# Feed-forward in row tiles of 64: the products with w1 and w3 side by side in two phases, the product with w2 in two parts, transposes in halves

## The chip, the cores and the metric

The kernel runs on one core of a Trainium2 chip. The metric is the device time of one execution in microseconds (us); three runs of the kernel before gave a median of 1179.75 us (1178.96 to 1179.86). A core has TensorE (PE in the profile; PEld is its weight load), VectorE (DVE), ScalarE (ACT), GpSimd (POOL) and SyncE (SP), which here only issues DMAs. Each engine works through its own instructions in the order of the program; between engines there are semaphores. Matrix products go to PSUM, eight banks of 128 partitions by 512 fp32 values, from which ACT and DVE read.

## The reference

A transformer block on x of 2048 rows by D = 448, 16 heads of 28 with one shared key and value, and a gated feed-forward of width F = 1792.

```python
x = A_x
h = x + _A_ref(_layernorm(x, axis=-1), A_wq, A_wk, A_wv, A_wo)
h2 = h + _B_ref(_layernorm(h, axis=-1), B_w1, B_w3, B_w2)

def _B_ref(x, w1, w3, w2):
    gate = jnp.einsum("bsd,df->bsf", x, w1)
    up = jnp.einsum("bsd,df->bsf", x, w3)
    h = _silu(gate) * up
    return jnp.einsum("bsf,fd->bsd", h, w2)
```

`_A_ref` is softmax attention over all 2048 keys; `_layernorm` has no gain or bias.

## The kernel before

**Numbers.** Operands of large products are fp32 values split into a rounded part and a remainder of the type fp32r (names ending in h and l, or index 0 and 1). A product is then three matmuls: high by high, low by high, high by low. D = 448 is three blocks of 128 and one of 64. For the last block the transposed input `xh[:, 3]` holds the low part in partitions 0 to 63 and the high part in 64 to 127, and the weights hold the same 64 rows twice, so that two matmuls over all 128 partitions do what three halves ask for. A product over D is thus 3 x 3 + 2 = 11 matmuls (`mm_D`, line 156).

**Stages.** The attention takes the span up to about 742 us; the change leaves its instructions alone on every engine. Then comes the feed-forward: 4 row tiles of T = 512 rows (t) by 14 chunks of 128 hidden columns (k), 56 iterations. One iteration, in the order in which the engines get it:

- `split_w(k+2)`: DVE copies the raw w1 and w3 of a later chunk into fp32r (line 442), POOL makes the remainder (line 443). The results are the tiles `qs`.
- `ffn1(t, k)`, line 970: two products of 11 matmuls, first w1 by the normalised input (`xh`, `xl`) into a bank `pa`, then w3 into another. Then the **hidden chain**: ACT Silu of the first bank (line 975), DVE multiplies with the second (977), ACT rounds the result (980), DVE makes the remainder (981). The tiles are `pt`, from a ring of four.
- what the table `after` hangs on this place: normalising the rows of the next tile (DVE, line 210), their transposes (`ln_tr`, line 238, 4 matmuls of 128x128 on PE, then ACT line 240 and DVE line 247), and in the first tile the last rows of the attention's output product (`wo_rows`).
- `ffn2` of the iteration before, line 989: 4 row blocks (n) by 3 matmuls of 128x448 into four banks Y, which are summed over all 14 chunks of a row tile.
- after chunk 0 of the next tile, `y_out` (993): DVE adds the four Y banks to the rows X, and a DMA writes them out.
- `split_w2(k+1)`: DVE line 455, POOL line 456, tiles `w2s`.

So `ffn2` of a chunk runs a whole `ffn1` later than the hidden chain that feeds it. Seven PSUM banks are handed out by `bank()`, which takes the free one that a small planner (`Clock`) expects to be ready first; the eighth (`po`) belongs to the attention.

**Row groups.** PE can be used by groups of its rows. The attention does it with 32 rows (lines 283 and 367, shown as 32*128): four matmuls, each on 32 partitions and into its own bank, follow each other within hundredths of a us. The feed-forward before uses all 128 rows (128*128) everywhere.

Of the kernel before, what the change touches and what calls it, by code (L numbers as in the profile page):

```python
# [35 lines left out]
def block_kernel(  # L36
# [18 lines left out]
    def f(ap):  # L55
        return ap.bitcast(F32)
# [81 lines left out]

    clock, ready = Clock(), {}
    free, used = list(range(7)), {}  # L140
    order = [0.0] * 7

    def bank(name="pb"):
        k = min(free, key=lambda k: order[k])
        free.remove(k)
        ps = ps_w.tile([P, T], F32, name=name, tag=f"bank{k}")
        used[id(ps)] = ps, k
        ready.pop(id(ps), None)
        return ps
# [65 lines left out]
    def xt_tiles():  # L215
        return [xt_pool.tile([P, m, T], F32R, name=name) for m, name in ((4, "xh"), (3, "xl"))]
# [11 lines left out]
    def ln_tr(t, c, spare=False):  # L228
        ps = last = TB[c] if TB else bank()
        if c == 0:  # L230
            XT[t] = xt_tiles()
        xh, xl = XT[t]
        r, c0 = (slice(0, P), c * P) if c < 3 else (slice(64, P), D - P)
        xns = LN[t][3]
        for n in range(NQ):
            if TB:
                break
            pe.transpose(ps[:, n * P : (n + 1) * P], xns[n][:, c0 : c0 + P], ident)  # L238
            clock.mm("full", 0, ps, 0.109, n == 0)
        se.activation(xh[r, c], ps[r], AF.Copy)  # L240
# [539 lines left out]
    def pt_ring():  # L780
        k, n_ring[0] = n_ring[0] % 4, n_ring[0] + 1
        return pt_new(k)
# [183 lines left out]

    HID, Y = {}, {}
    o_norm(NG - 1)

    def ffn1(t, k, W):  # L970
        ps = [bank("pa"), bank("pa")]
        for m in range(2):
            mm_D(ps[m], ps[m], [w[:, :, 1 - m] for w in W], XT[t], slice(0, P), slice(0, T))
        sg = f(pt_ring()[:, 0])
        se.activation(sg, ps[0], AF.Silu)  # L975
        done(ps[0])
        ve.tensor_tensor(sg, ps[1], sg, op=ALU.mult)  # L977
        done(ps[1])
        h = pt_ring()
        se.activation(h[:, 0], sg, AF.Copy)  # L980
        ve.tensor_tensor(h[:, 1], sg, f(h[:, 0]), op=ALU.subtract)  # L981
        HID[t, k] = h[:, 0], h[:, 1]

    def ffn2(t, k, n):
        if n == 0 and k == 0:
            Y[t] = [bank() for _ in range(NQ)]
        hid, w2s = HID[t, k], WS[t, k]
        for m, (a, b) in enumerate(((0, 0), (1, 0), (0, 1))):
            pe.matmul(Y[t][n][:, :D], hid[a][:, n * P : (n + 1) * P], w2s[:, b, :D],  # L989
                      start=(k == 0 and m == 0), stop=(k == NF - 1 and m == 2))  # L990

    def y_out(t, n):
        ve.tensor_tensor(X[t][:, n], Y[t][n][:, :D], X[t][:, n], op=ALU.add)  # L993
# [7 lines left out]
    after = {}  # L1001

    def on(t, k, fn, *args):
        after.setdefault((t, k), []).append((fn, args))

    on(0, 0.5, o_mul, tl, NG - 1)
    on(0, 2, o_split, tl, NG - 1, lambda o, i: se.activation(o, i, AF.Copy), ve)
    for k in range(2):
        on(0, 2.5, load_w13, 2 * tl + k)
    for n in range(NQ):  # L1010
        on(0, 3 + n / 2, wo_rows, tl, n)
        on(0, 5 + n, ln_stats, tl, n)
    on(0, 4.5, put_late)
    for k in range(8, NF):
# [3 lines left out]
    for t in range(1, NT):  # L1018
        for n in range(NQ):
            on(t - 1, 1 + n, ln_norm, t, n)  # L1020
        for c in range(4):
            on(t - 1, 5 + c, lambda t, c: ln_tr(t, c), t, c)

    prev = None
    for t in range(NT):
        for k in range(NF):
            end = t == tl and k >= NF - 2
            t2, k2 = divmod(NF * t + k + 2, NF)
            if t2 < NT:
                WH[t2, k2] = split_w(k2)  # L1030
            ffn1(t, k, WH.pop((t, k)))
            for fn, args in after.get((t, k), []):
                fn(*args)
            if prev is not None and not end:
# [8 lines left out]
            for fn, args in after.get((t, k + 0.5), []):  # L1043
                fn(*args)
            prev = (t, k)
    for n in range(NQ):
        ffn2(tl, NF - 3, n)
# [34 lines left out]
```

## Time and profile before

| | us |
|---|---|
| median of 3 runs | 1179.75 |
| the profiled execution | 1180.76 |
| its span | 1179.0 |
| PE busy in the span | 1168.7 |
| DVE, ACT, POOL busy in the span | 784.5, 745.1, 325.3 |
| PE busy between 900 and 1000 us (feed-forward) | 100.0 |
| DVE, ACT, POOL busy there | 37.8, 17.8, 49.4 |
| granted PE clock, mean of the span | 1.00 |

Rows of the groups view give line, engine, operation, output<-input and count, then busy time and mean ns of one, then the idle time before them and who ended it. Rows of the timeline give the start in us, the duration in us, engine, line and operation; equal neighbours are merged, with their count. A matmul's duration there is longer than the distance to the next one, because matmuls are pipelined: what counts is the distance between starts.

### The profile page before, as it was taken

The page shows a single profiled execution, that of the slowest core. Times are in us where ns is not written, and L with a number is a line of the kernel's source. Part 1 is how long each engine was busy: PE and PEld are TensorE (multiplying, and loading weights), DVE is VectorE, ACT ScalarE, POOL GpSimd, SP SyncE. Part 2 cuts the span into 40 slices and gives each one's busy share as a digit, 9 for nine tenths or more (in the row PEclk, how much of TensorE's full clock was granted, in tenths as well). Part 3 has the DMA queues.
Part 4 walks back from the last instruction along what each step waited for, and adds up shares of the span by engine and source line. Part 5 has one row for each costly group of instructions (what it writes and reads, how often), then busy time and mean ns, then how long its engine had stood idle before and what let it go on. Part 6 is the DMA issues. An engine that isn't in the chain of part 4 may idle for free.

```text
span 1179.0 us, 22184 instructions
## 1 busy us (share of the span) xinstructions
PE 1168.7 (99%) x8618; PEld 748.5 (63%) x8618; DVE 784.5 (67%) x1479; ACT 745.1 (63%) x1435; POOL 325.3 (28%) x240
## 2 busy tenths in 40 slices
PE   8999999999999999999999999999999999999998
PEld 6664444445444445444455443788888888888887
DVE  7878999897899988989987961454343333333332
ACT  5649999996999997999997999312112211211111
POOL 5312001111110111110113013335555445455552
PEclk9999999999999999999999999999999999999999
DMA  4010100011000001000011000242000000000000
GB/s 165 10 37 1 42 10 11 19 22 39 19 19 5 16 24 38 19 19 13 9 39 35 6 18 19 70 113 69 1 32 1 1 4 28 1 1 32 1 1 31
DMA packets 35049, 30.58 MB, mean 26 GB/s; under 512 B 11904, under 2 KB 29568, under 8 KB 34944
## 3 DMA queue, kind: packets, MB, share of 16 engines
q1 hardware_dynamic: 34944, 29.17, 8.6%
q8 instruction: 67, 1.10, 0.4%
q14 instruction: 38, 0.31, 0.1%
HBM read 20.37 MB, written 3.80 MB: 20 GB/s over the span
## 4 chain that ended last, share of the span: by engine, by line
PE 93%; ACT 2%; DVE 2%; DMA 1%; issue 1%; SPq 0%; POOLq 0%; POOL 0%; ACTq 0%; DVEq 0%
PE pa L163 26%; PE po L383 21%; PE pb L367 20%; PE pb L989 11%; PE pa L283 10%; PE pb L163 4%; PE pb L238 1%; ACT OT L390 1%; DVE mx L293 1%; ACT ab L304 1%; ACT pt L374 0%; DMA sd<-sm 0%; DMA X<-in_A_x_dram 0%; DVE pt L981 0%; DVE X L993 0%
## 5 line engine op out<-in xcount | busy, mean ns | idle before, releaser
L293 DVE TENSOR_REDUCE mx<-pa 128x1 f32<-128x512 f32 x689 | 440.4, 685 | 21.9 <-PE pb L367 12.9
L367 PE MATMUL pb<-qs,KS 32*128 32x512 f32 x3072 | 385.3, 425 | 0.0
L374 ACT ACTIVATE pt<-pb 128x512 f32<-128x512 f32 x684 | 365.9, 620 | 12.5 <-PE pb L367 9.4
L367 PEld LDWEIGHTS pb<-qs,KS 32*128 32x128 f32 x3072 | 233.9, 182 | 133.4 <-ACT pt L374 68.1
L283 PE MATMUL pa<-KS,qs 32*128 32x512 f32 x886 | 312.1, 459 | 1.4
L163 PE MATMUL pa<-xh,qs 128*128 128x512 f32 x896 | 231.2, 390 | 0.0
L283 PEld LDWEIGHTS pa<-KS,qs 32*128 32x128 f32 x886 | 138.9, 182 | 82.8 <-DVE mx L293 46.4
L163 PEld LDWEIGHTS pa<-xh,qs 128*128 128x128 f32 x896 | 168.1, 188 | 33.8 <-issue 0.8
L383 PE MATMUL po<-pt,VA 128*32 128x512 f32 x1368 | 182.2, 604 | 0.4 <-ACT pt L374 0.4
L977 DVE TENSOR_TENSOR pt<-pa,pt 128x512 f32<-128x512 f32 x56 | 38.7, 691 | 206.9 <-PE pa L163 202.3
L975 ACT ACTIVATE pt<-pa 128x512 f32<-128x512 f32 x56 | 33.5, 599 | 193.0 <-PE pa L163 193.0
L989 PE MATMUL pb<-w2s,pt 128*128 128x448 f32 x660 | 144.4, 367 | 1.0 <-DVE pt L981 0.8
L414 POOL TENSOR_TENSOR OT<-OT,rb 128x512 f32<-128x512 f32 x15 | 19.2, 1282 | 456.3 <-DMA rb<-sd 251.6
L980 ACT ACTIVATE pt<-pt 128x512 fp32r<-128x512 f32 x56 | 35.4, 632 | 153.6 <-DVE pt L977 149.4
L989 PEld LDWEIGHTS pb<-w2s,pt 128*128 128x128 f32 x660 | 122.9, 188 | 13.4 <-DVE pt L981 1.2
L311 DVE CUSTOM_DVE_ANT_0 ab<-pa,ab 128x512 f32<-128x512 f32 x138 | 93.7, 687 | 39.8 <-PE pa L283 32.6
L374 ACT ACTIVATE xl<-pb 128x512 f32<-128x512 f32 x170 | 99.5, 609 | 7.6 <-PE pb L367 5.5
L374 ACT ACTIVATE xh<-pb 128x512 f32<-128x512 f32 x170 | 104.2, 631 | 0.0
L163 PE MATMUL pa<-xl,qs 128*128 128x512 f32 x336 | 94.5, 389 | 0.0
L383 PE MATMUL po<-xh,VA 128*32 128x512 f32 x340 | 89.4, 605 | 0.0
L383 PE MATMUL po<-xl,VA 128*32 128x512 f32 x340 | 89.4, 605 | 0.0
L304 ACT ACTIVATE ab<-pa 128x512 f32<-128x512 f32 x138 | 82.3, 608 | 6.6 <-PE pa L283 4.8
(109 smaller groups left out, 1088.8 us busy)
## 6 DMA issues: line engine op xcount, KB each, us to landing
rb<-sd SPq DMA_DIRECT2D x64, 64.0 KB
QR<-OT SPq DMA_DIRECT2D x60, 56.0 KB
QR<-in_B_w_dram SPq DMA_DIRECT2D x16, 192.0 KB
X<-in_A_x_dram SPq DMA_DIRECT2D x3, 896.0 KB
out_dram<-X SPq DMA_DIRECT2D x3, 896.0 KB
w<-in_B_w_dram SPq DMA_DIRECT2D x8, 192.0 KB
w_wo<-in_B_w_dram SPq DMA_DIRECT2D x6, 224.0 KB
qs<-mr SPq DMA_DIRECT2D x64, 2.0 KB
```

The source lines that it names most:

```text
L163: pe.matmul(ps, lhs[b][:, cb, lsl], rhs[a][:, ca, rsl], start=(k == 0), stop=(k == len(terms) - 1),)
L283: pe.matmul(ps, QS[i][r, 0, n * P : (n + 1) * P], KS[0][r, kt * T : (kt + 1) * T] if keys is None else keys[r], start=True, stop=True)
L293: ve.tensor_reduce(self.to(), ps, axis=AX.X, op=ALU.max)
L304: se.activation(self.ab, ps, AF.Relu)
L311: ve.tensor_tensor_reduce(self.ab, ps, self.ab, 1.0, -3.0e38, ALU.add, ALU.max, self.to())
L367: pe.matmul(self.ps, KS[k % 2][r, c * P : (c + 1) * P], QS[i][r, k // 2], start=(k == 0), stop=(k == 2))
L374: se.activation(f(PT[i, c, p][:, jj]), self.ps, AF.Exp, bias=0.0, scale=SCALE)
L383: pe.matmul(PO[i][32 * j : 32 * j + 32], VA[:, c], f(PT[i, c, j // 2][:, j % 2]), start=(c == 0), stop=(c == NC - 1))
L975: se.activation(sg, ps[0], AF.Silu)
L977: ve.tensor_tensor(sg, ps[1], sg, op=ALU.mult)
L980: se.activation(h[:, 0], sg, AF.Copy)
L989: pe.matmul(Y[t][n][:, :D], hid[a][:, n * P : (n + 1) * P], w2s[:, b, :D], start=(k == 0 and m == 0), stop=(k == NF - 1 and m == 2))
```

## The change

All iterations from chunk 4 of the first row tile (`FULL = 4`) up to chunk 11 of the last, 10 + 14 + 14 + 12 = 50 of the 56, use PE in two row groups of 64. A matmul on partitions 0 to 63 and one on 64 to 127 are issued in turn (`two`).

- `ffn1` becomes an early and a late phase. Early, the lower half works on w1 into bank 0 and the upper half on w3 into bank 1; late, each half works on the other bank. The last block of D no longer needs its doubled form in each phase: early there are 11 matmuls to a half, late 10. The early phase needs the high part of the last block in partitions 0 to 63 too, which `put_xd` copies once per row tile (ACT) to a tile named `rb`.
- `ffn2` is cut the same way: early, the lower half adds to Y 0 and 2 and the upper to 1 and 3; late they swap. The order within an iteration is now ffn1 early, ffn2 early, ffn1 late, ffn2 late.
- Between the phases stands `settle`: ACT reads one element of a bank that was just written, and the matmul that next writes to that bank waits for it.
- The hidden chain starts when the late phase ends. After chunk 0 of a tile it is interrupted by the late half of `ffn2` and `y_out`.
- The transposes are done in halves of 64 rows (`tr_half`), two blocks at a time, in chunks 5 and 7 of the tile before.
- In `y_out` of the first three tiles, two of the four adds go from DVE to ACT (a copy out of PSUM, line 1078) and POOL (the add).
- The bank `po` joins the pool as an eighth bank; `wo_rows` moves from chunks 3 to 4.5 to chunks 3 and 3.5, ahead of the first half iteration.

```diff
+    free.append(7)
+    order[7] = clock.end + 4
...
+    HALF = (slice(0, 64), slice(64, 128))
+    PAIRS3 = ((0, 0), (1, 0), (0, 1))
+    FULL = 4
+    XD = {}
+
+    def put_xd(t):
+        if not XD:
+            XD[0] = wk_pool.tile([P, T], F32R, name="rb")
+        se.activation(XD[0][:64], f(XT[t][0][64:, 3]), AF.Copy)
+
+    def two(pairs):
+        for units in zip(*pairs):
+            for h, (ps, lhs, rhs, first, last) in enumerate(units):
+                pe.matmul(ps[:, : rhs.shape[-1]], lhs, rhs, start=bool(first), stop=bool(last), skip_group_check=True)
+                clock.mm("half", h, ps, 0.016 + rhs.shape[-1] / 2400, first)
+
+    def settle(ps):
+        se.activation(pexp[:1, 8:9], ps[:1, :1], AF.Copy)
+
+    def hidden(t, k, ps, then=None):
         sg = f(pt_ring()[:, 0])
         se.activation(sg, ps[0], AF.Silu)
         done(ps[0])
         ve.tensor_tensor(sg, ps[1], sg, op=ALU.mult)
         done(ps[1])
+        if then is not None:
+            then()
         h = pt_ring()
         se.activation(h[:, 0], sg, AF.Copy)
         ve.tensor_tensor(h[:, 1], sg, f(h[:, 0]), op=ALU.subtract)
         HID[t, k] = h[:, 0], h[:, 1]
...
+    def products(t, W, m, h):
+        r = HALF[h]
+        u = [(W[b][r, c, 1 - m], XT[t][a][r, c]) for a, b in PAIRS3 for c in range(3)]
+        return u + [(W[0][r, 3, 1 - m], XT[t][0][r, 3])]
+
+    def ffn1_half(t, k, W, ps, late):
+        us = [products(t, W, late, 0), products(t, W, 1 - late, 1)]
+        if not late:
+            extra = W[1][HALF[0], 3, 1], XD[0][HALF[0]]
+            us[0].insert(0 if k == NF - 1 else len(us[0]), extra)
+            us[1].append((W[1][HALF[1], 3, 0], XT[t][0][HALF[1], 3]))
+        to = (ps[0], ps[1]) if not late else (ps[1], ps[0])
+        two([[(to[h], *u, not late and x == 0, late and x == len(us[h]) - 1) for x, u in enumerate(us[h])]
+             for h in range(2)])
+        if not late:
+            settle(ps[1])
...
+    def ffn2_half(t, k, late):
+        if k == 0 and not late:
+            Y[t] = [bank() for _ in range(NQ)]
+        hid, w2s = HID[t, k], WS[t, k]
+        us = [[], []]
+        for h in range(2):
+            for n0 in (2, 0) if late else (0, 2):
+                n, r = n0 + (h ^ late), HALF[h]
+                for m, (a, b) in enumerate(PAIRS3):
+                    us[h].append((Y[t][n], hid[a][r, n * P : (n + 1) * P], w2s[r, b, :D],
+                                  not late and k == 0 and m == 0, late and k == NF - 1 and m == 2))
+        two(us)
+        settle(Y[t][0 if late else 3])
...
     def y_out(t, n):
-        ve.tensor_tensor(X[t][:, n], Y[t][n][:, :D], X[t][:, n], op=ALU.add)
+        y, eng = Y[t][n][:, :D], ve
+        if t < NT - 1 and n > 1:
+            y, eng = ln_pool.tile([P, 512], F32, name="xn", bufs=4)[:, :D], ge
+            se.activation(y, Y[t][n][:, :D], AF.Copy)
+        eng.tensor_tensor(X[t][:, n], y, X[t][:, n], op=ALU.add)
...
-            ffn1(t, k, WH.pop((t, k)))
-            for fn, args in after.get((t, k), []):
-                fn(*args)
-            if prev is not None and not end:
-                for n in range(NQ):
-                    ffn2(*prev, n)
-                if prev[1] == NF - 1:
+            W = WH.pop((t, k))
+            if t == 0 and k < FULL or end:
+                ffn1(t, k, W)
+                call(after, t, k)
+                if prev is not None and not end:
                     for n in range(NQ):
-                        y_out(prev[0], n)
+                        ffn2(*prev, n)
+            else:
+                ps = [bank("pa"), bank("pa")]
+                ffn1_half(t, k, W, ps, 0)
+                call(between, t, k)
+                ffn2_half(*prev, 0)
+                ffn1_half(t, k, W, ps, 1)
+
+                def rest():
+                    ffn2_half(*prev, 1)
+                    call(behind, t, k)
+                    if prev[1] == NF - 1:
+                        for n in range(NQ):
+                            y_out(prev[0], n)
+
+                hidden(t, k, ps, rest if prev[1] == NF - 1 else None)
+                call(after, t, k)
+                if prev[1] != NF - 1:
+                    rest()
```

**The order on PE.** The first place is an ordinary iteration of the feed-forward. Before, on PE (`pa` are the two banks of ffn1, `pb` the banks of Y, `qs` weights, `xh` and `xl` the input; 128x512 is the output of one matmul):

```order
L163 MATMUL pa<-xh,qs 128x512 x3
L163 MATMUL pa<-xl,qs 128x512 x3
L163 MATMUL pa<-xh,qs 128x512 x8
L163 MATMUL pa<-xl,qs 128x512 x3
L163 MATMUL pa<-xh,qs 128x512 x5
L989 MATMUL pb<-w2s,pt 128x448 x12
```

There are 22 matmuls of 512 columns and 12 of 448, one after the other over all rows of PE. Now, at the same place (`rb` is the copy of the last block's high part), where each matmul uses 64 rows and neighbours use different halves:

```order
L992 MATMUL pa<-xh,qs 128x512 x6
L992 MATMUL pa<-xl,qs 128x512 x6
L992 MATMUL pa<-xh,qs 128x512 x8
L992 MATMUL pa<-rb,qs 128x512
L992 MATMUL pa<-xh,qs 128x512
L992 MATMUL pb<-w2s,pt 128x448 x12
L992 MATMUL pa<-xh,qs 128x512 x6
L992 MATMUL pa<-xl,qs 128x512 x6
L992 MATMUL pa<-xh,qs 128x512 x8
L992 MATMUL pb<-w2s,pt 128x448 x12
```

In pairs these are 11 + 10 pairs of 512 columns and 6 + 6 pairs of 448; ffn2 stands in two parts, one between the phases of ffn1 and one behind.

**The order on ACT and DVE after chunk 0 of a tile.** The second place is the iteration in which the Y banks of a finished tile are read out. On DVE before (977 multiplies, 981 makes the remainder, 993 adds Y to X):

```order
L977 TENSOR_TENSOR pt<-pa,pt 128x512
L981 TENSOR_TENSOR pt<-pt 128x512
L993 TENSOR_TENSOR X_77<-pb,X_77 128x448 x4
L455 CAST w2s<-w2r_100 128x448
L442 CAST qs<-QR_89 128x1024
```

and now, with the same operations on lines 1002, 1008 and 1079:

```order
L1002 TENSOR_TENSOR pt<-pa,pt 128x512
L1079 TENSOR_TENSOR X_77<-pb,X_77 128x448 x2
L1008 TENSOR_TENSOR pt<-pt 128x512
L462 CAST w2s<-w2r_100 128x448
L449 CAST qs<-QR_89 128x1024
```

On ACT now (1000 is Silu, 996 is settle, 1078 copies Y out of PSUM, 1007 rounds the hidden tile):

```order
L1000 ACTIVATE pt<-po 128x512
L996 ACTIVATE pexp<-pb 1x1
L1078 ACTIVATE xn<-pb 128x448 x2
L1007 ACTIVATE pt<-pt 128x512
L996 ACTIVATE pexp<-pa 1x1
L996 ACTIVATE pexp<-pb 1x1
```

The remainder on DVE and the rounding on ACT, which stood ahead of the read-out of Y, now stand behind half of it each.

More of the change, by code (lines that the diff above doesn't have):

```diff
@@ L982, in ffn1 @@
         HID[t, k] = h[:, 0], h[:, 1]
+    def ffn1(t, k, W):
+        ps = [bank("pa"), bank("pa")]
+        for m in range(2):
+            mm_D(ps[m], ps[m], [w[:, :, 1 - m] for w in W], XT[t], slice(0, P), slice(0, T))
+        hidden(t, k, ps)
+    def products(t, W, m, h):
[13 more added lines that the diff above has]
+            settle(ps[1])
     def ffn2(t, k, n):
@@ L1020, in block_kernel @@
             on(t - 1, 1 + n, ln_norm, t, n)
-        for c in range(4):
-            on(t - 1, 5 + c, lambda t, c: ln_tr(t, c), t, c)
+        for p in range(2):
+            for late in range(2):
+                on(t - 1, 5 + 2 * p, tr_half, t, (2 * p, 2 * p + 1), late, to=behind if late else between)
+        on(t - 1, NF - 1, put_xd, t, to=between)
     prev = None
@@ L1042, in block_kernel @@
                 WS[t2, k2] = split_w2(k2)
-            for fn, args in after.get((t, k + 0.5), []):
-                fn(*args)
+            call(after, t, k + 0.5)
             prev = (t, k)
```

51 lines of the change are left out of this document (37 added, 14 removed).

## The prediction

> **What bounds the kernel now.** I read the page first, the engines' shares and the chain of waits:
>
> ```profile
> PE 1168.7 (99%) x8618; PEld 748.5 (63%) x8618; DVE 784.5 (67%) x1479; ACT 745.1 (63%) x1435; POOL 325.3 (28%) x240
> PE 93%; ACT 2%; DVE 2%; DMA 1%; issue 1%; SPq 0%; POOLq 0%; POOL 0%; ACTq 0%; DVEq 0%
> ```
>
> PE is the chain. A busy PE need not be a full one, so next came windows: one of the attention and one of the feed-forward (columns: stretch, its length, then PE, PEld, DVE, ACT, POOL, clock, DMA share, GB/s).
>
> ```profile
> 100.00:700.00 600.00, 598.62 (x5681) 294.83 (x5679) 533.89 (x1001) 568.24 (x1121) 72.32 (x72) 1.00 0.08 21
> 900.00:1000.00 100.00, 100.00 (x464) 85.73 (x463) 37.81 (x67) 17.79 (x30) 49.38 (x26) 1.00 0.03 10
> ```
>
> In the feed-forward PE runs at full clock while DVE, ACT and POOL work half of the time at most. One iteration in the timeline:
>
> ```profile
> 947.19 0.86 PE L163 MATMUL pa<-xh,qs 128*128 128x512 f32 x3
> 947.25 0.40 DVE L455 CAST w2s<-w_wo 128x448 fp32r<-128x448 f32 x1
> 949.22 2.40 POOL L443 TENSOR_TENSOR qs<-QR,qs 128x1024 fp32r<-128x1024 f32 x1
> 949.96 0.60 ACT L975 ACTIVATE pt<-pa 128x512 f32<-128x512 f32 x1 [3.57 <-PE pa L163]
> 952.19 2.60 PE L989 MATMUL pb<-w2s,pt 128*128 128x448 f32 x12
> 952.46 0.69 DVE L977 TENSOR_TENSOR pt<-pa,pt 128x512 f32<-128x512 f32 x1 [4.21 <-PE pa L163]
> 953.19 0.63 ACT L980 ACTIVATE pt<-pt 128x512 fp32r<-128x512 f32 x1 [2.63 <-DVE pt L977]
> 953.85 0.69 DVE L981 TENSOR_TENSOR pt<-pt 128x512 fp32r<-128x512 f32 x1 [0.70 <-ACT pt L980]
> 954.62 0.86 PE L163 MATMUL pa<-xh,qs 128*128 128x512 f32 x3
> ```
>
> From start to start the 22 matmuls of ffn1 take 952.19 - 947.19 = 5.00 us, 0.227 each, and the 12 of ffn2 take 2.43 us, 0.2025 each. PE waits for nothing: an iteration is 7.43 us because 34 matmuls must be issued. The hidden chain ends at 954.54 and its result is first read a whole ffn1 later, at 954.62 + 5.00; that slack of 5 us is what the change spends.
>
> **The removed matmul.** An iteration has 11 + 10 + 6 + 6 = 33 pairs in place of 34 matmuls. If a pair takes as long as one full matmul, each iteration saves 0.227 us, and 50 iterations 11.4 us. Two conditions stand behind this: the halves must run side by side, and a pair must cost no more. No 64-row group is in this trace; the nearest rows are the attention's 32-row groups, four at a time, on PE at the end of the attention:
>
> ```profile
> 728.08 0.97 PE L367 MATMUL pb<-qs,KS 32*128 32x512 f32 x12
> 728.98 0.62 PE L383 MATMUL po<-xh,VA 128*32 128x512 f32 x2
> 731.86 1.42 PE L367 MATMUL pb<-qs,KS 32*128 32x512 f32 x16
> 733.21 1.06 PE L383 MATMUL po<-pt,VA 128*32 128x512 f32 x8
> ```
>
> Twelve, three on each group, take 0.90 us until the next kind of work starts. One after another they would take 12 x 0.227 = 2.7, so groups do run side by side. Of the sixteen, five are on one group (H2 on line 946), and they take 1.35: two more rounds for 0.45, or 0.225 each. The starts are rounded to 0.01, which makes that 0.215 to 0.235. I take 0.226 for a pair, between this and the full matmul's 0.227, and 1.3 ns less for the narrower pairs as well: 1650 pairs give 2.1 us. Halfway to the ends of what rounding allows, 0.2235 to 0.2295, the term goes from -6 to +4 us.
>
> **Issue.** PE now has 132 instructions in an iteration (66 matmuls, 66 weight loads) in place of 68. The attention window shows 5681 + 5679 in 600 us, 0.0528 us each; 132 of these take 6.97 us, less than the 7.16 that an iteration should last. So issue is hidden, though with little to spare.
>
> **The settle waits.** ACT answers on a bank while PE does other work. After the early ffn1 this work is six pairs of ffn2, 6 x 0.2025 = 1.215 us; before the other answers are due, ten pairs and more. In the rows above ACT and DVE start 0.27 us after the last matmul's slot ends (952.46 against 952.19). For a tiny operation on ACT the nearest row is
>
> ```profile
> L468 ACT ACTIVATE pexp<-pexp 128x8 f32<-128x8 f32 x1 | 0.2, 208 | 0.0
> ```
>
> so the answer is there after 0.27 + 0.21 + 0.06 = 0.54 us. Even a whole-bank copy (0.60) in its place would be done after 0.93. I cost it at nothing; without the cover it would be 0.54 twice in an iteration. ACT is in order, so a settle also stands behind the rounding of the hidden tile, which the next term times; behind a settle itself stand the next settle, the copies of the transposes and the next Silu, none of which is due sooner. Behind the waiting matmul stands all of PE, so every late answer would count in full.
>
> **The hidden chain.** Call T the end of the late phase. Both banks end together now, so Silu no longer runs under the second product. With the gaps of the rows above: Silu from T + 0.27, multiply from T + 0.91, rounding from T + 1.64, remainder from T + 2.30 to 2.99; PE sees it at T + 3.05. The settle on Y behind the rounding is done by T + 2.5. PE has the late ffn2 (1.215) and the early ffn1 of the next iteration (11 x 0.227 = 2.50) to do, is at ffn2 at T + 3.72, and at its second pair, which is the first to read the remainder, at T + 3.92. The slack falls from 5 us to 0.87, and an ordinary iteration waits for nothing. Banks: four Y, two for this iteration, two of the last, which are free by T + 1.7; with transposes in the iteration these two are taken, and the next ffn1, due at T + 1.65 or later, meets the multiply's end at T + 1.60. The difference is too small to count.
>
> **After chunk 0, three times.** Here the chain is interrupted. ACT waits for the late ffn2 (T + 1.22), settles (to T + 1.70) and copies two banks; DVE adds two. Nearest rows for the copy, the adds on DVE, and POOL at 448 columns:
>
> ```profile
> L599 ACT ACTIVATE OS<-OT 128x448 fp32r<-128x448 f32 x2 | 1.0, 560 | 0.0
> L993 DVE TENSOR_TENSOR X<-pb,X 128x448 f32<-128x448 f32 x16 | 9.1, 618 | 1.9 <-PE pb L989 1.9
> 773.92 1.16 POOL L456 TENSOR_TENSOR w2s<-w_ks,w2s 128x448 fp32r<-128x448 f32 x1 [1.94 <-PE pb L989]
> ```
>
> The copies end at T + 2.83, the rounding at T + 3.47, the remainder would run to T + 4.2: 0.3 us late for PE. But POOL adds from about T + 2.4 to 4.7, and these rows of the first chunks show what DVE does when it starts a remainder while POOL works:
>
> ```profile
> 763.13 2.40 POOL L443 TENSOR_TENSOR qs<-QR,qs 128x1024 fp32r<-128x1024 f32 x1
> 763.46 2.62 DVE L981 TENSOR_TENSOR pt<-pt 128x512 fp32r<-128x512 f32 x1 [0.70 <-ACT pt L980]
> ```
>
> DVE ended 0.55 us after POOL did. If that goes for the pair of adds, the remainder ends at T + 5.25 and PE waits 1.4 us; if DVE gets in between the two, 0.4. I take the middle of 0.3 and 1.4, three times, 2.5 us; the ends are 1 and 4 us.
>
> The Trainium skill, page "SBUF — State Buffer", section "Who interferes with whom", says that a DVE instruction with two SBUF inputs and a GpSimd instruction that reads SBUF lock each other out, and that the first to issue keeps the lock for one whole instruction. By that DVE comes in after the first add and the term is some 1.3 us. The two rows show the lock, but not who goes first between two POOL instructions.
>
> **Smaller edits.** Transposes: 4 in an iteration cost 901.02 to 908.97 less 7.43, 0.52 us,
>
> ```profile
> 901.02 0.87 PE L163 MATMUL pa<-xh,qs 128*128 128x512 f32 x3
> 908.97 0.86 PE L163 MATMUL pa<-xh,qs 128*128 128x512 f32 x3
> ```
>
> and twelve such groups 6.2. There are now twelve groups of 4 pairs, each loading the same 128 columns of weights; I take the same price, with half of it (-3 us) as one end and +1 as the other. Changing from full rows to halves and back happens twice; in the burst at 728.08 three rounds took 0.90 where 3 x 0.225 = 0.68 would do, so 0.2 a change, 0.4 us in all. The copy of `rb` (four of about 0.6 on ACT) runs between phases on an idle ACT. `wo_rows` does the same matmuls one iteration earlier, and the loads that wait for its tiles may start sooner. The attention is unchanged.
>
> **Sum**, against the profiled execution: 1180.76 - 11.4 - 2.1 + 2.5 + 0.4 = 1170.2. The median of the runs lies 1.0 below the profiled one, so 1169.2 us.
>
> **Rivals.**
>
> *The hidden chain is late in every iteration (slower).* If POOL's L443 (2.40) falls on the remainder each time, as at 763.13, the remainder takes up to 2.62 in place of 0.69, 1.93 more; less the slack of 0.87 PE waits 1.06 us in the 44 iterations that have no transposes to wait under, 47 us, and the time is about 1216. It decides from a wait of 0.25 us an iteration. For it: the chain is now exposed. Against: L443 follows the cast of w2s, by 949.22 + 2.40 - 947.25 = 4.37 us, and that cast comes after the remainder; so it ends near T + 7.4, two us before the next remainder.
>
> *PE cannot issue twice the instructions at this rate (slower).* From 7.43 / 132 = 0.0563 us an instruction on, the halves lose; at 0.060 an iteration takes 7.92 us, 0.49 more than before, 24 us in all, and the time is about 1204. For it: the attention's mean of 0.0528 is only 6% below that point. Against: the attention had to wait for its other engines too, so its mean is no limit.
>
> The Trainium skill, page "TensorE: Matmul & The Clock Gate", section "Wait — 56ns, not 53.3ns?", gives about 62 ns for each matmul where the sequencer decodes it. By that 66 matmuls, 4.1 us, stay hidden; if a weight load cost as much, this rival would hold with an estimated 8.2 us an iteration. The 0.0528 of the trace disagrees with the latter.
>
> *Given back.* Waits of 0.1 to 0.25 us in each iteration, from settles or banks that the planner chose badly, would return 5 to 12 us: 1174 to 1181. Against it: the slacks of 0.7 and 0.87 above.
>
> *Better than forecast.* A pair at 0.224, the cheap end of the transposes and 1 us for the three interruptions: 1163 to 1165. For it: the rounding of the burst's rows leaves room for such a pair, and half a transpose has half the columns to stream.
>
> **How the numbers follow.** The forecast 0.60, better 0.21, given back 0.09, the chain 0.06, issue 0.04. Two runs of this kernel can be told apart from about 0.2%, 2.4 us; so faster needs 1177.4 or less: forecast, better and a third of "given back", 0.83; same 0.06; slower 0.11. The range takes the unknown slot (-6 to +4), the interruptions and the transposes together: 1163.5 to 1176.5.
>
> **What would show it.** Right: matmuls 64*128 in pairs; an iteration of about 7.16 to 7.20 us without transposes; PE idle only after chunk 0 of tiles 1 to 3, released by the remainder (line 1008), about 0.8 us each time; settles (line 996) of about 0.2 us that PE never waits for. Wrong: a pair of more than 0.23 us, PE idle in ordinary iterations, DVE remainders of over 0.7 us there, or no side-by-side running at all.

## The result, and the profile after

| | before | after |
|---|---|---|
| median of 5 runs each, us | 1179.75 | 1168.77 |
| lowest and highest, us | 1178.96 to 1180.05 | 1168.19 to 1169.37 |
| the profiled execution, us | 1180.76 | 1168.84 |
| its span, us | 1179.0 | 1167.0 |

The ratio is 0.9908, with a 95% interval of 0.9898 to 0.9919: faster by 0.9%. The forecast was 1169.2 us. It lies 0.4 us from the median, but the terms of its sum were less exact than that, as the accounting below shows.

Engine shares and the chain of waits, on the page after:

```profile
PE 1156.8 (99%) x10266; PEld 758.7 (65%) x10266; DVE 781.1 (67%) x1473; ACT 768.6 (66%) x1595; POOL 334.0 (29%) x246
PE 93%; DVE 2%; ACT 2%; DMA 1%; issue 1%; SPq 0%; POOL 0%; POOLq 0%; ACTq 0%; DVEq 0%
```

PE is still the chain, with 10266 matmuls in place of 8618. The window of the feed-forward after (columns as in the prediction):

```profile
900.00:1000.00 100.00, 100.00 (x932) 94.98 (x931) 35.75 (x62) 24.53 (x73) 55.79 (x30) 1.00 0.03 10
```

PE takes twice the instructions (932 matmuls for 464), at the same full clock and without idle time. An ordinary iteration in the timeline after, with the last step of the hidden chain, the remainder, on DVE (line 1008; other rows left out):

```profile
932.44 0.97 PE L992 MATMUL pb<-w2s,pt 64*128 64x448 f32 x7
933.65 0.91 PE L992 MATMUL pa<-xh,qs 64*128 64x512 f32 x6
934.72 0.69 DVE L1008 TENSOR_TENSOR pt<-pt 128x512 fp32r<-128x512 f32 x1 [0.70 <-ACT pexp L996]
936.17 0.36 PE L992 MATMUL po<-w2s,pt 64*128 64x448 f32 x1
936.37 0.37 PE L992 MATMUL po<-w2s,pt 64*128 64x448 f32 x1
937.38 0.92 PE L992 MATMUL pa<-xh,qs 64*128 64x512 f32 x6
938.76 1.13 PE L992 MATMUL pa<-xh,qs 64*128 64x512 f32 x8
939.67 0.97 PE L992 MATMUL pb<-w2s,pt 64*128 64x448 f32 x7
940.88 0.92 PE L992 MATMUL pa<-xh,qs 64*128 64x512 f32 x6
```

Read the phases by their first starts. Early ffn1 goes from 933.65 to 936.17, 2.52 us for 11 pairs; early ffn2 to 937.38, 1.21 for 6; late ffn1 to 939.67, 2.29 for 10; late ffn2 to 940.88, 1.21. The iteration is 7.23 us; it was 7.43. On average a pair of 512 columns takes 0.229 us and one of 448 takes 0.202. The late phase ended at T = 932.44, and the remainder ended at T + 2.97 (935.41), while the first pair that reads it starts at 936.37. That leaves 0.96 us, or 0.90 with the 0.06 that the prediction allows between a result and its reader; the prediction said 0.87.

An iteration with transposes (line 1066), in the timeline after:

```profile
785.74 0.86 PE L992 MATMUL pa<-xh,qs 64*128 64x512 f32 x6
788.26 0.21 PE L1066 MATMUL po<-ident,xn 64*128 64x64 f32 x1
788.32 0.22 PE L1066 MATMUL po<-ident,xn 64*128 64x64 f32 x1
788.48 1.45 PE L992 MATMUL pb<-w2s,pt 64*128 64x448 f32 x12
793.65 0.96 PE L992 MATMUL pa<-xh,qs 64*128 64x512 f32 x6
796.28 1.37 PE L992 MATMUL pb<-w2s,pt 64*128 64x448 f32 x12
```

It takes 7.91 us, 0.68 more than a plain one, and the early ffn1 behind it 2.63 in place of 2.52: 0.79 us for two blocks of four transposes. Before, two blocks cost 2 x 0.52.

The iteration after chunk 0 of a tile, where Y is read out between the multiply and the rounding (1078 the copies out of PSUM, 1079 the adds on POOL, of which the row at 861.72 shows the second alone):

```profile
860.01 0.94 ACT L1078 ACTIVATE xn<-pb 128x448 f32<-128x448 f32 x2
860.61 2.71 POOL L1079 TENSOR_TENSOR X<-xn,X 128x448 f32<-128x448 f32 x2 [2.19 <-ACT xn L1078]
860.86 0.61 ACT L1007 ACTIVATE pt<-pt 128x512 fp32r<-128x512 f32 x1
861.51 0.80 DVE L1008 TENSOR_TENSOR pt<-pt 128x512 fp32r<-128x512 f32 x1 [0.22 <-ACT pt L1007]
861.72 1.59 POOL L1079 TENSOR_TENSOR X<-xn,X 128x448 f32<-128x448 f32 x1
862.14 0.36 PE L992 MATMUL po<-w2s,pt 64*128 64x448 f32 x1
862.23 1.34 DVE L462 CAST w2s<-w2r 128x448 fp32r<-128x448 f32 x1
863.48 0.86 PE L992 MATMUL pa<-xh,qs 64*128 64x512 f32 x6
```

POOL is at its two adds from 860.61 to 863.32. DVE starts the remainder at 861.51, within them, and it takes 0.80, not 2.62. The cast behind it takes 1.34 in place of 0.39, and ends 0.25 us after POOL. So DVE got in between the two adds: the second, which began at 861.72, took 1.59 in place of the 1.16 of such an instruction before, and the cast had to wait for its end. The early ffn2 takes 1.34 us (862.14 to 863.48) in place of 1.21.

**Where the 12.0 us between the two spans are**, from the starts of the phases:

| part | forecast | measured |
|---|---|---|
| 50 iterations, 7.43 to 7.23 us | -13.5 | -10.0 |
| transposes, six times 0.79 - 1.04 | 0 | -1.5 |
| after chunk 0 (early ffn2 1.34, 1.38 and 1.35) | +2.5 | +0.4 |
| changes between full rows and halves | +0.4 | +0.4 |
| ahead of the first half iteration | 0 | -1.3 |
| sum | -10.6 | -12.0 |

The last term has two parts, and neither is of the change's making. The attention ended earlier: the first ffn2 starts at 751.53, before at 752.26. And the wait of PE for a remainder in chunk 1 was shorter (0.3 us for 0.8 in the waits view; that ffn2 lasted 3.01 us for 3.51). The attention and the chunks up to this place have the same instructions in every kernel of this study, and in their profiles that start lies anywhere from 751.3 to 754.2 and that ffn2 lasts from 2.49 to 3.51. So 1.2 us of the 12.0 are variation between executions, and the 10.8 that are left fit the 11.0 between the medians. The same 1.2 would account for the 1.0 us by which the profiled execution of the kernel before stood above its median; that was not shown.

### The profile page after: what moved, and what is told of

Same layout as the page of the kernel before. It is cut to its first block, busy times and chain, and to the rows that moved or that the text cites. A ratio compares the mean times of both kernels' runs of the same rounds, so it can differ in the third digit from the quotient of the medians.

```text
span 1167.0 us, 25723 instructions
## 1 busy us (share of the span) xinstructions
PE 1156.8 (99%) x10266; PEld 758.7 (65%) x10266; DVE 781.1 (67%) x1473; ACT 768.6 (66%) x1595; POOL 334.0 (29%) x246
## 4 chain that ended last, share of the span: by engine, by line
PE 93%; DVE 2%; ACT 2%; DMA 1%; issue 1%; SPq 0%; POOL 0%; POOLq 0%; ACTq 0%; DVEq 0%
PE po L390 21%; PE pb L374 20%; PE pa L992 18%; PE pa L290 10%; PE pb L992 9%; PE pa L166 4%; PE pb L166 4%; PE po L992 4%; ACT OT L397 1%; DVE mx L300 1%; ACT ab L311 1%; PE pb L240 1%; PE pb L1039 1%; ACT pt L381 0%; DMA sd<-sm 0%
## 5 line engine op out<-in xcount | busy, mean ns | idle before, releaser
L992 PE MATMUL pa<-xh,qs 64*128 64x512 f32 x1262 | 206.9, 389 | 0.0
L1002 DVE TENSOR_TENSOR pt<-pa,pt 128x512 f32<-128x512 f32 x50 | 34.5, 691 | 181.1 <-ACT pt L1000 174.8
L992 PEld LDWEIGHTS pa<-xh,qs 64*128 64x128 f32 x1262 | 147.6, 184 | 12.0
L992 PE MATMUL pb<-w2s,pt 64*128 64x448 f32 x1050 | 139.3, 363 | 0.0
L992 PEld LDWEIGHTS pb<-w2s,pt 64*128 64x128 f32 x1050 | 116.5, 184 | 6.3 <-DVE pt L1008 0.4
L1000 ACT ACTIVATE pt<-pa 128x512 f32<-128x512 f32 x48 | 28.7, 598 | 93.4 <-PE pa L992 89.0
L992 PE MATMUL pa<-xl,qs 64*128 64x512 f32 x522 | 87.1, 388 | 0.0
L450 POOL TENSOR_TENSOR qs<-QR,qs 128x1024 fp32r<-128x1024 f32 x32 | 76.5, 2392 | 15.0 <-DVE qs L449 9.8
```

Of the source, the lines that this page charges most:

```text
L450: ge.tensor_tensor(wl, W13[k], f(wh), op=ALU.subtract)
L992: pe.matmul(ps[:, : rhs.shape[-1]], lhs, rhs, start=bool(first), stop=bool(last), skip_group_check=True)
```

## The experiments

Each kernel is the changed one with one edit, compared with runs of the kernel before on the same chip. "Above the change" is against its 1168.77; the kernel before had medians of 1179.44 to 1180.08 beside these runs, so differences of half a us are not resolved.

### Does the gain come from the removed slot?

**One pair more.** The late phase issues its last pair twice, so it has 11 pairs and the iteration 34. The last product of each half is counted twice in the sums.

```diff
         if not late:
             ...
+        else:
+            for u in us:
+                u.append(u[-1])
```

> The changed kernel with an eleventh pair in each late phase (the last product of each half is added a second time, so the sums differ from the reference). Theory A: the gain is the one matmul slot that an iteration no longer issues, and PE is the bound; 50 pairs at the 0.229 us that the trace of after shows give +11.5 us, about 1180.2, and a plain iteration of 7.46 us. Rival B: the gain comes from the other edits (eighth bank, split read-out of Y, rows of wo earlier) and PE has slack in the halves; then the extra pair is partly hidden and the time stays under 1175.

Measured: 1180.61 us, ratio 1.0003 (0.9994 to 1.0013), 11.8 above the change. Its timeline:

```profile
926.56 0.87 PE L992 MATMUL pa<-xh,qs 64*128 64x512 f32 x6
934.01 0.87 PE L992 MATMUL pa<-xh,qs 64*128 64x512 f32 x6
```

An iteration takes 7.45 us in place of 7.23. One pair in each iteration is the whole gain; give it back and the kernel is where it was.

**All rows, everything else kept.** All 56 iterations run `ffn1` and `ffn2` over 128 rows again and the transposes stand in their old places; the eighth bank, the moved `wo_rows` and the read-out of Y on ACT and POOL stay.

```diff
-            if t == 0 and k < FULL or end:
+            if True:
...
+                    if prev[1] == NF - 1:
+                        for n in range(NQ):
+                            y_out(prev[0], n)
```

> All edits but the halves: eighth bank, the read-out of Y split between DVE and ACT with POOL, rows of wo earlier; ffn1, ffn2 and the transposes use all rows as before. Theory A: the kernel before again, 1178.5 to 1180 (half a us may be left from the shorter wait in chunk 1). Rival B: most of the gain stays, 1172 or less.

Measured: 1180.17 us, ratio 0.9997 (0.9988 to 1.0007). The other edits bring nothing by themselves.

### Must the two halves alternate?

**Late phase not in turn.** All ten matmuls of the lower half, then all ten of the upper; the other phases keep the old order (`turn`). This is a single run, without an interval.

```diff
-    def two(pairs):
-        for units in zip(*pairs):
-            for h, (ps, lhs, rhs, first, last) in enumerate(units):
+    def two(pairs, turn=True):
+        units = [(h, u) for h in range(2) for u in pairs[h]]
+        if turn:
+            units = [(h, u[h]) for u in zip(*pairs) for h in range(2)]
+        if units:
+            for h, (ps, lhs, rhs, first, last) in units:
...
-             for h in range(2)])
+             for h in range(2)], not late)
```

> In the late phase the ten matmuls of the lower half are issued first, then the ten of the upper half, in place of in turn. Theory A: matmuls start in the order of issue and a half cannot start its next one before its last has streamed, so the halves run one after the other: 10 more slots of 0.229 in 50 iterations, +114 us, about 1283. Rival: PE overlaps row groups by itself, whatever the order, and the time stays near 1169.

Measured: 1221.49 us, 52.7 above the change, 1.05 us an iteration on average and 0.88 in a plain one (8.11 for 7.23). Neither theory: one after the other would cost 10 pairs' time, 2.3 us, and free running nothing. The timeline of one late phase, where the lower half writes `pa` and the upper `po`:

```profile
1001.87 0.39 PE L995 MATMUL pa<-xh,qs 64*128 64x512 f32 x1
...
1003.27 0.39 PE L995 MATMUL pa<-xh,qs 64*128 64x512 f32 x1
1003.27 0.49 PE L995 MATMUL po<-xh,qs 64*128 64x512 f32 x1
...
1003.95 0.39 PE L995 MATMUL pa<-xh,qs 64*128 64x512 f32 x1
...
1004.77 0.47 PE L995 MATMUL pb<-w2s,pt 64*128 64x448 f32 x1
...
1005.46 0.39 PE L995 MATMUL po<-xh,qs 64*128 64x512 f32 x1
```

The matmul at 1003.27 on `pa` is the seventh of the lower half. With it starts the first of the upper half, which stands eleventh in the program: it overtakes the eighth, ninth and tenth, of which the last starts at 1003.95. At the other end the lower half has gone on to ffn2 (1004.77) while the upper has ffn1 matmuls left until 1005.46; when this first ffn2 matmul starts, three matmuls that stand ahead of it have again not started. So PE did not start these matmuls in the order of the program, as the opening has it for every engine; a matmul on the other half of the rows went up to three places ahead of the oldest that had not started. The Trainium skill, page "TensorE: Matmul & The Clock Gate", section "Part 3: Packing small matmuls — row/col tiling", says that matmuls start and end in the order of the program and are not reordered. These rows differ.

**Blocks of five**, to test the three places: five of the lower half, five of the upper, and again (`step` is 5 in the late phase of ffn1 and 1 elsewhere).

```diff
-    def two(pairs):
...
+    def two(pairs, step=1):
+        units = [(h, u) for i in range(0, len(pairs[0]), step) for h in range(2) for u in pairs[h][i : i + step]]
...
-             for h in range(2)])
+             for h in range(2)], 5 if late else 1)
```

> The late phase in blocks: five matmuls of the lower half, five of the upper, five of the lower, five of the upper. Asked by the run with ten and ten, which cost 1.05 us an iteration where strict order of issue gives 2.3. Theory W: PE starts a matmul of the other half up to three places ahead of the oldest one that has not started (in the run with ten and ten the eleventh matmul started with the seventh); then blocks of five run one slot apart and cost 0 to 0.25 us an iteration: 1169 to 1181. Theory S, strict order: the blocks overlap only at their seams, 17 slots in place of 10, 7 x 0.229 x 50 = +80 us, about 1249.

Measured: 1174.19 us, ratio 0.9949 (0.9933 to 0.9966), 5.4 above the change, 0.1 us an iteration on average. A plain iteration loses only 0.02 (7.25 for 7.23, from the starts of Silu); the rest lies in the iterations with transposes (7.71 and 8.09 for 7.53 and 7.72) and after chunk 0 (7.70 for 7.33). That is within what a window of three places gives and far from strict order. The gain needs the two halves near each other in the program, not strictly in turn. The length of the window is inferred from these two orders alone.

### What of the slacks?

**One step more in the hidden chain.** ACT copies the product of the multiply onto itself before it rounds it.

```diff
-    def hidden(t, k, ps, then=None):
+    def hidden(t, k, ps, then=None, more_acts=0):
...
+        for _ in range(more_acts):
+            se.activation(sg, sg, AF.Copy)
         h = pt_ring()
...
-                hidden(t, k, ps, rest if prev[1] == NF - 1 else None)
+                hidden(t, k, ps, rest if prev[1] == NF - 1 else None, 1)
```

> One more operation in the hidden chain of the 50 half iterations: ACT copies the product onto itself (0.63 us) between the multiply and the rounding. Theory: slack of 0.9 us (forecast 0.87) falls to 0.25 and plain iterations do not change; only the three iterations after chunk 0, which wait already, pay 0.66 each: +2 us, 1170 to 1171.5. Rival: the slack is smaller than the arithmetic says, or POOL's 2.4 us instruction falls on the remainder now: +10 us or more.

Measured: 1172.53 us, ratio 0.9937 (0.9922 to 0.9952), 3.8 above the change, where 2 was expected. Plain iterations still take 7.23. What it costs lies after chunk 0:

```profile
861.85 2.26 POOL L1081 TENSOR_TENSOR X<-xn,X 128x448 f32<-128x448 f32 x2 [1.52 <-ACT xn L1080]
863.41 1.24 DVE L1010 TENSOR_TENSOR pt<-pt 128x512 fp32r<-128x512 f32 x1 [0.88 <-ACT pt L1009]
864.71 0.47 PE L992 MATMUL pb<-w2s,pt 64*128 64x448 f32 x1 [0.80 <-DVE pt L1010]
```

POOL's second add had begun when the remainder was due at 863.41. It took 1.24 in place of 0.69 and ended 0.54 after POOL did. The early ffn2 took 2.39 us (863.44 to 865.83) in place of the change's 1.34; three times 1.05 is 3.2 of the 3.8. This is the case that the prediction feared for the change itself, at 1.4 us each: the remainder behind both adds.

**Two steps more**: the same with 2 as the last argument.

> Two such copies, 1.32 us more in the chain. Theory: PE waits 0.4 us for the remainder in some 41 iterations and 1.3 in three: +16 to +22 us, 1185 to 1191, so slower than the kernel before. Rival: the slack is larger (the remainder could come later than the second pair), under 1173.

Measured: 1192.59 us, ratio 1.0109 (1.0092 to 1.0126), 23.8 above the change. In a plain iteration:

```profile
929.04 0.69 DVE L1010 TENSOR_TENSOR pt<-pt 128x512 fp32r<-128x512 f32 x1 [2.03 <-ACT pexp L996]
929.19 0.39 PE L992 MATMUL pb<-w2s,pt 64*128 64x448 f32 x1
929.79 0.47 PE L992 MATMUL pb<-w2s,pt 64*128 64x448 f32 x1 [0.20 <-DVE pt L1010]
930.91 0.86 PE L992 MATMUL pa<-xh,qs 64*128 64x512 f32 x6
```

The remainder ends at 929.73 and the second pair starts at 929.79, where 0.20 after the first would be 929.39: a wait of 0.40, of which the row prints 0.20. The early ffn2 takes 1.72 us in place of 1.21, 0.51 more, so PE loses 0.11 beyond the wait itself. Two copies of 0.65 less a slack of 0.90 are this 0.40. The slack of the plain iteration is real, and it is less than 1.3.

**Four answers in place of one** after the early ffn1 (line 996):

```diff
         if not late:
-            settle(ps[1])
+            for _ in range(4):
+                settle(ps[1])
```

> The settle after the early phase of ffn1 is done four times in a row on ACT (0.16 us each in the trace of after), so its answer comes after 0.27 + 0.64 + 0.06 = 0.97 us, or sooner if the four overlap. The early part of ffn2 covers 1.21 us. Theory: no change, 1168 to 1169.5, PE idle nowhere new. Rival: the wait is already at its limit, and each 0.1 us more costs 50 x 0.1 = 5 us: 0.48 us more would be +24 us, 1193.

Measured: 1171.16 us, ratio 0.9922 (0.9904 to 0.9941), which overlaps the change's. PE waits for none of the answers, and a plain iteration takes 7.25 at a granted clock of 0.997 (7.23 at 1.000 in the change). In the profiled execution the feed-forward started 2.6 us later than in the change's (754.16).

**Eight answers:**

> The same settle eight times: the answer after 0.27 + 1.28 + 0.06 = 1.61 us against 1.21 of cover. Theory: PE waits 0.4 us in the 44 iterations without transposes in between and 0.1 in the six with them: +18 us, about 1187 (less if settles overlap on ACT). Rival: something else covers it (ACT ahead, PE queue), under 1172.

Measured: 1202.60 us, ratio 1.0196 (1.0179 to 1.0213), 33.8 above the change, where 18 was expected.

```profile
965.46 0.36 PE L992 MATMUL po<-w2s,pt 64*128 64x448 f32 x1
965.74 1.50 ACT L996 ACTIVATE pexp<-pa 1x1 f32<-1x1 f32 x8 [1.77 <-PE pa L992]
967.30 0.96 PE L992 MATMUL pa<-xh,qs 64*128 64x512 f32 x6 [0.45 <-ACT pexp L996]
969.70 0.57 PE L992 MATMUL pb<-w2s,pt 64*128 64x448 f32 x4
```

Eight answers take 1.50, 0.188 each, where 0.16 had been counted (each writes the same element and waits for the one before); they start 0.28 after the early ffn1 ended, and PE goes on 0.06 behind them. That is 1.84 us in place of 1.21, so a wait of 0.63. The late ffn1 behind it takes 2.40 in place of 2.29: after a wait PE loses 0.11 more. At 0.74 the 33.8 us are 46 of the 50 iterations; those with transposes have more cover. By the same sum one answer is there after 0.28 + 0.16 + 0.06 = 0.50 us, and four after 1.09, both under the cover of 1.21.

### What do the pieces around it cost?

**Transposes over all rows** again, one block at a time, as before the change.

```diff
-        for p in range(2):
-            for late in range(2):
-                on(t - 1, 5 + 2 * p, tr_half, ...)
+        for c in range(4):
+            on(t - 1, 5 + c, lambda t, c: ln_tr(t, c), t, c)
```

> Transposes over all rows again, one block in each of chunks 5 to 8, while ffn1 and ffn2 stay in halves. Theory A: each of the 12 groups costs its 0.52 us of before and two changes between full rows and halves of together 0.2 to 0.45 us, as the two changes in the trace of after cost (0.20 in, 0.24 out); the halves cost 0.79 for two blocks, 4.7 us in all. So 8.6 to 11.6 in place of 4.7: +4 to +7 us, 1173 to 1176. Rival: a change of row groups costs nothing that shows, and the transposes cost as in the kernel before, 6.2 us: +1.5 us, 1170.3.

Measured: 1173.56 us, ratio 0.9940 (0.9926 to 0.9955), 4.8 above the change.

```profile
902.17 0.39 PE L992 MATMUL pa<-xh,qs 64*128 64x512 f32 x1
904.55 0.66 PE L240 MATMUL pb<-ident,xn 128*128 128x128 f32 x4
910.20 0.39 PE L992 MATMUL pa<-xh,qs 64*128 64x512 f32 x1
```

An iteration with them takes 8.03, 0.80 more; twelve are 9.6 us, and six times 0.79 are 4.7: the difference of 4.9 is near the 4.8 measured. Before the change the same four transposes cost 0.52. The other 0.28 is left for going to full rows and back between two half phases.

**ffn2 over all rows**, in one part between the phases (and one more small read on ACT in the transposes, which keeps their order):

```diff
-                ffn2_half(*prev, 0)
+                for n in range(NQ):
+                    ffn2(*prev, n)
                 ffn1_half(t, k, W, ps, 1)
...
-                    ffn2_half(*prev, 1)
```

> ffn1 in two phases of halves, but ffn2 over all rows, whole, between the phases; nothing stands behind the late phase. The transposes stay in halves. Theory: two changes of row groups in each iteration at together 0.44 us (0.20 and 0.24 in the trace of after), and the chain, which now has only the early ffn1 as cover (2.52 + 0.1 + 0.2 against 3.05), waits 0.2 us more: 50 x 0.44 = 22 to 50 x 0.64 = 32 us, 1191 to 1201, slower than the kernel before. Rival: changes of row groups are free, and only the chain waits: 1169 to 1180.

Measured: 1209.71 us, ratio 1.0252 (1.0234 to 1.0269), above the forecast.

```profile
939.63 0.69 DVE L1008 TENSOR_TENSOR pt<-pt 128x512 fp32r<-128x512 f32 x1 [0.70 <-ACT pt L1007]
940.00 2.88 PE L1039 MATMUL pb<-w2s,pt 128*128 128x448 f32 x12
940.38 2.12 PEld L1039 LDWEIGHTS pb<-w2s,pt 128*128 128x128 f32 x11 [0.20 <-DVE pt L1008]
947.80 2.88 PE L1039 MATMUL pb<-w2s,pt 128*128 128x448 f32 x12
```

An iteration takes 7.80, 0.57 more, 28.5 us in 50. Two costs are in it. One is the two changes of row groups, which took 0.44 once in and once out in the change and 0.28 around the transposes. The other is a wait for the remainder, whose cover is now the early ffn1 alone: the remainder ends at 940.32, and the second weight load of ffn2, which reads it, starts at 940.38. Behind the transposes of the run before this one, without such a wait, the second matmul followed the first by 0.31; here it follows by 0.38. The waits view has 38 waits of weight loads for the remainder (first row of the next view). The run does not separate the two costs; with 0.44 for the changes, 0.13 an iteration is left for the wait. The other 12.4 are waits for banks, at the transposes and for the remainder after chunk 0. The waits view of the whole span (total, times, longest):

```profile
PEld pb L1039 <- DVE pt L1008: 11.8, 38, 1.4
PE pa L992 <- DVE pt L1002: 7.0, 6, 1.2
PE pb L1039 <- DVE pt L1008: 3.9, 4, 1.1
PE pb L1066 <- DVE xn L213: 1.7, 3, 0.6
```

The three rows of PE are together 12.6, of which the wait in chunk 1 is no part of the edit. Halves for ffn1 alone would be slower than no halves: that ffn2 is cut too removes no matmul, but spares the two changes and puts six more pairs between the hidden chain and its reader.

**The chain not interrupted** after chunk 0: `hidden` runs to its end, then the late ffn2 and `y_out`.

```diff
-                hidden(t, k, ps, rest if prev[1] == NF - 1 else None)
+                hidden(t, k, ps)
                 call(after, t, k)
-                if prev[1] != NF - 1:
-                    rest()
+                rest()
```

> After chunk 0 the hidden chain is no longer interrupted: rounding and remainder come first, then the late ffn2's settle and the read-out of Y. Theory: the wait of 0.13 to 0.17 us that PE has there in the trace of after goes (0.45 us in all), and the banks of Y are still free in time (about T + 4.2 against T + 4.3): 1168.2 to 1168.8, the difference not resolved by the times, but PE without those waits in the trace. Rival: the banks of Y come late, and PE waits 0.5 to 1 us three times: 1170 to 1172.

Measured: 1168.89 us, ratio 0.9912 (0.9897 to 0.9927): the same. The early ffn2 there takes 1.22 us, so the wait of 0.13 is gone, and nothing came in its place that the time could show. The interruption was not needed.

**All four adds on DVE:**

```diff
-        if t < NT - 1 and n > 1:
+        if False:
```

> All four adds of Y to X on DVE again, in the middle of the chain as in the change (ACT and POOL take none). Theory: the remainder comes behind four adds of 0.6 us from T + 1.75, at T + 4.2 to 4.9, against T + 3.92: PE waits 1.0 us three times in place of 0.15: +2.6 us, 1171 to 1172. Rival: the split between engines was not needed, the same time within 0.5 us.

Measured: 1170.28 us, ratio 0.9921 (0.9907 to 0.9936), 1.5 above the change.

```profile
860.10 2.22 DVE L1079 TENSOR_TENSOR X<-pb,X 128x448 f32<-128x448 f32 x4
862.24 0.68 DVE L1008 TENSOR_TENSOR pt<-pt 128x512 fp32r<-128x512 f32 x1
```

Four adds hold the remainder up until 862.24 (861.51 in the change) and the early ffn2 takes 1.99 in place of 1.34: 0.65 three times, 2.0 us. The times differ by less than their intervals, but the rows show the wait. No kernel of the study beat the change.

## Why the prediction was right, and where its terms were not

**The bound and the removed slot: right.** PE does nothing but issue matmuls there, and a pair is worth 0.22 us an iteration (7.45 against 7.23): the extra pair took back all of the gain, and full rows with all the other edits gained nothing. The halves run side by side, as it was read off the attention's bursts.

**The pair: mis-sized.** The step that failed is "I take 0.226 for a pair, between this and the full matmul's 0.227, and 1.3 ns less for the narrower pairs as well". A pair of 512 columns takes 0.229 on average, more than a full matmul, and one of 448 takes 0.202, less than 1 ns under a full one. The iteration came out at 7.23, outside the 7.16 to 7.20 that should have shown the forecast right, and the term lost 3.5 us: 2.1 for the cheaper pair that was not there, and 1.4 because pairs were dearer than full matmuls. The dear ones are the first of each phase. Start by start in the trace after, the pairs from the fifth on lie 0.227 apart, as full matmuls do, and the first four 0.228 to 0.236 (medians between 900 and 1000 us): in the late phase above the six pairs from 937.38 take 0.230 each, the four from 938.76 0.2275. The first three full matmuls of an ffn1 before took 0.23 each as well, but ffn1 now begins twice in an iteration. Why the first ones are slower was not settled.

The estimate was the difference of two bursts of 0.90 and 1.35 us divided by two rounds, so the difference between their ends is in it. With windows that begin inside a burst, the timeline before shows the rounds themselves, 0.23 apart:

```profile
728.42 0.64 PE L367 MATMUL pb<-qs,KS 32*128 32x512 f32 x8
728.65 0.40 PE L367 MATMUL pb<-qs,KS 32*128 32x512 f32 x4
```

The bounds 0.2235 and 0.2295 don't come out of the working that the prediction names, which would give 0.2205 and 0.2305; the value lies within both.

It is not issue that made the pairs dear: in ffn2 24 PE instructions pass in 1.21 us, 0.050 each, while in ffn1 44 take 2.52, 0.057 each. That also refutes the second rival, by which PE could not issue so many.

**The interruptions: mis-sized, the mechanism right.** The prediction took the middle between DVE getting in between POOL's two adds and waiting for both. It gets in, and its remainder was ready for it 0.4 us sooner than reckoned: the two copies on ACT began at T + 1.60 for T + 1.70 and took 0.94, not 2 x 0.56, the rounding began before they ended, and it ended at T + 3.06 rather than T + 3.47 (861.47 against 858.41, the start of the late ffn2). So 0.4 us for all three in place of 2.5. The Trainium skill, page "SBUF — State Buffer", section "Who interferes with whom", has the lock held for one whole instruction. The trace agrees: the remainder slipped in at 861.51 and the cast behind it was held until the second add ended; with one more copy ahead of it the remainder fell into the second add and took 1.24.

**The transposes: mis-sized.** "I take the same price" was wrong by 1.5 us, and the end of -3 was nearer. Four pairs of half transposes start 0.06 apart and let ffn2 start 0.22 after the first (788.26 to 788.48), while four full ones with equal weight loads cost 0.52: that fits a price that goes with the 64 columns that each streams, not with its weights.

**The changes of row groups: right**, 0.20 into the halves and 0.24 out, 0.4 in all. But it is cheap only because it happens twice; made in each iteration, the two changes and the wait that came with them cost 0.57, more than the gain of 0.20.

**Costed at nothing: right.** The settles, up to four of them, hide under the early ffn2. The hidden chain has 0.90 us to spare. One copy more doesn't touch a plain iteration, two cost 23.8 us and make the kernel slower than before. So the first rival priced a real danger: a remainder 0.40 us too late loses twice what the change gains. It did not come about, because the remainders of plain iterations met no POOL instruction and took 0.69. "Given back" needed waits in each iteration, and there are none.

The errors, +3.5, -2.1, -1.5 and the -0.3 left of the part ahead once the 1.0 between profile and median is taken off, cancel to -0.4. That the forecast was better than its parts is luck; the range, which was built from their bounds, is what the working really supported. Three figures of the prediction don't follow from its terms: the three bounds added up give 1160.8 to 1177.8, a little more than the stated range; "better than forecast" with all three of its conditions gives 1161.4, not 1163 to 1165; and the chances add to 0.84 faster and 0.10 slower.

## What to carry to other kernels

Where an engine does nothing but issue, count the slots: one slot in 34 was the whole gain, and it could be read off an iteration's row and one extra-pair run. Row groups pay only if matmuls of different groups stand near each other in the program and if whole stretches stay in them, since two changes in an iteration (0.28 and 0.44 us here) cost more than the removed slot. When a change spends a slack, lengthen the chain by known steps until PE waits: that gives the slack in two runs, and shows the places (here after chunk 0) that have less of it than the rest.

## What the runs showed of the hardware that was not expected

- PE started a matmul of the other 64 rows up to three places ahead of the oldest one not started: with ten in a row on one half a plain iteration lost 0.88 us, not 2.3; with five, 0.02.
- A change from 64-row groups to full rows and back cost 0.28 us on top of the transposes; once in and once out, 0.20 and 0.24. Around ffn2 in each iteration it cost less than 0.57, which holds a wait as well.
- Two 64-row matmuls side by side went at the pace of one full matmul, 0.227 us for 512 columns, after the first four of a phase, which took 0.228 to 0.236.
- A wait of PE cost about 0.1 us more than its length: the phase behind it took 2.40 in place of 2.29.
- Between two POOL instructions that follow each other DVE got in, and the second POOL instruction waited for it (1.59 us, and 2.71 for the two; 2.26 where DVE was late).
- ACT operations on a single element took 0.16 us alone, and 0.188 each in a row of eight of which each waits for the one before.
